# A list-scheduled attention and MLP kernel: opening reordered, MLP tiles put forward, second weights in three pieces, last tile split 512+256 on two queues

## The chip, the cores and the metric

The kernel runs on one core of a Trainium2 chip. The metric is the device time of one execution in microseconds (us), as the median of several executions. "Half clock" below means stretches in which the record of the granted TensorE clock is below 1.0; in the trace before it was 0.5 in one such stretch of 3.4 us, from 22.14 to 25.55 us. All runs of this case are on one core, and none was put into a slower state than "fast".

## The reference

```python
# q, k, v: (8, 12, 448, 64) float32;  x: 3584 x 768;  w_in: 768 x 2048;  w_out: 2048 x 768
scores = (1 / sqrt(64)) * q @ k.T                  # per batch and head, 448 x 448
attn   = maximum(scores, 0) ** 2 / 448 @ v
x      = attn.transpose(0, 2, 1, 3).reshape(3584, 768)
h      = x @ w_in
g      = 0.5 * h * (1 + erf(h / sqrt(2)))          # exact gelu
out    = g @ w_out                                 # float32
```

## The kernel before

All matrix products are in bf16; the loads cast on the way (float32 inputs, bf16 tiles). A scheduler written in Python fixes the order of each engine's instructions when the kernel is built. In the trace before TensorE kept to it: it stood 1.28 us, up to 20.45, before transposes whose keys had not landed, with other work behind them. The scheduler keeps a model of when each engine comes free, when a load lands and when a buffer is released, and issues next the operation whose modelled start plus a bias is lowest. So a changed bias, or a changed model of a load, changes the order on every engine. Once the attention of batch 2 begins, TensorE's order is a fixed list that mixes attention of one batch with the MLP of the two before.

```python
T_BIAS = -0.5      # transposes of queries and keys
T_LATE = 0.2       # ... of the second half of batch 0's queries
F1_BIAS = 0.2      # MLP tiles of the first half of batch 0
F1B_BIAS = 0.2
RELU_DVE = 0.36    # extra cost of relu on DVE instead of ACT
DMA_FREE = 4.0
LEAD = 5           # MLP tiles of batch 1 ahead of the first scores of batch 2
...
    def commit(self, est, op, eng, dur, lat):        # in class Scheduler
        if eng == "PE" and est < self.COLD: dur, lat = 2 * dur, 2 * lat    # COLD = 18.0
        if isinstance(lat, tuple):                   # a load: (bytes, count)
            t = max(self.dma, est + dur + 1.0)
            self.dma = t + lat[0] / 390e3
            op.done = self.dma + DMA_LAT
...
    sch = Scheduler({"w": 3, "a": NA, "f": 2, "osb": 3})    # score, square, MLP, output buffers
...
    # warm-up of TensorE, before anything has landed
    spin = w_pp.tile([128, 2, NB], F32, tag="w", name="spin")
    for _ in range(45):
        nc.tensor.matmul(spin[:, 0, :128], zero, zero, start=True, stop=True)
...
    # one pair of score blocks: TensorE -> "ps"; ACT (or DVE) relu -> "a_sq"; DVE squares it
            A.activation(ar, ps, AF.Relu, scale=c_att)       # or V.tensor_scalar(...)
            V.tensor_mul(box["a2"][:, :, :used], ar, ar)
...
    # batch 2: permute on DVE, transpose by DMA, and a gate that holds back later loads
    for g in range(G):
        add_pk(2, g, g + 1, bias=T_TWO)
        add_pq(2, g, g + 1, bias=T_TWO)
    add_T_dma(2, [[]] * 7)
    add_gate(2)
    add_wout(0)                                      # second weights, first half
    add_wout(1)                                      # ... second half
...
    # an output tile: 128 tokens x 768, as two halves of 384 (ND), stored by SP
    for kf in range(KF):
        nc.tensor.matmul(po[:, :ND], hT[pr][:, kf, bass.ts(t, 128)],
                         wout_sb[:, kf, bass.ts(n, ND)], start=(kf == 0), stop=(kf == KF - 1))
    copy(e, osbs[pr, t][:, bass.ts(n, ND)], box[0][:, :ND])
    ...
    nc.sync.dma_start(rows[c, p0 : p0 + m, :], osbs[pr, t][...])
```

Names in the profile: `tp` are transposes on TensorE of queries `nq` and keys `nk`, `ps` scores, `pav` the attention product, `psh` the first MLP product and `pso` the second. Batches 0 and 1 are transposed on TensorE, later ones by DMA (`kT<-pk`, `qT<-pq`).

## Time and profile before

| | before |
|---|---|
| time, median of 3 | 396.78 us (396.65 to 398.15) |
| profiled execution | span of 395.7 us, of which TensorE is busy 381.9 |
| last copy ends, to the end of the span | 391.27, 4.4 us |

The page of a profile gives busy times and 40 slices of the span. The waits of an engine list what ended its idle time. The timeline gives, in order, start, duration, engine, line and tile of each group, with the idle time before it in brackets. The lines on which the argument rests are shown in the prediction below. In the trace before, 16 matmuls of 384 columns take 2.60 us, 162.5 ns each (the last copies of 384 columns start at 388.11 and 390.71), and the issue of a store takes about 0.4 us.

### The profile page before, as it was taken

The page shows a single profiled execution, that of the slowest core. Times are in us where ns is not written, and L with a number is a line of the kernel's source. Part 1 is how long each engine was busy: PE and PEld are TensorE (multiplying, and loading weights), DVE is VectorE, ACT ScalarE, POOL GpSimd, SP SyncE. Part 2 cuts the span into 40 slices and gives each one's busy share as a digit, 9 for nine tenths or more (in the row PEclk, how much of TensorE's full clock was granted, in tenths as well). Part 3 has the DMA queues.
Part 4 walks back from the last instruction along what each step waited for, and adds up shares of the span by engine and source line. Part 5 has one row for each costly group of instructions (what it writes and reads, how often), then busy time and mean ns, then how long its engine had stood idle before and what let it go on. Part 6 is the DMA issues. An engine that isn't in the chain of part 4 may idle for free.

```text
span 395.7 us, 8091 instructions
## 1 busy us (share of the span) xinstructions
PE 381.9 (97%) x3497; PEld 218.1 (55%) x3497; DVE 187.5 (47%) x346; ACT 200.5 (51%) x306; POOL 45.2 (11%) x68
## 2 busy tenths in 40 slices
PE   7689999999999999999999999999999999999994
PEld 6467684455455555555555555555555555555562
DVE  3868963267737345555456345545355352111111
ACT  4969956763534564465635456356626545222200
POOL 8665204000200200020000200000000000000000
PEclk9989999999999999999999999999999999999999
DMA  9999956999996792579119871370111011110122
GB/s 174 194 202 204 200 94 105 211 204 207 159 195 132 116 193 54 112 135 184 42 42 164 125 140 41 65 156 2 42 30 51 0 41 41 40 39 2 41 80 80
DMA packets 69347, 42.94 MB, mean 109 GB/s; under 512 B 37696, under 2 KB 65728, under 8 KB 69312
## 3 DMA queue, kind: packets, MB, share of 16 engines
q0 software_dynamic: 30496, 22.47, 38.2%
q1 hardware_dynamic: 38544, 19.51, 22.5%
q8 instruction: 27, 0.44, 0.4%
q10 hardware_dynamic: 272, 0.46, 0.3%
q14 instruction: 8, 0.07, 0.0%
HBM read 45.61 MB, written 11.01 MB: 143 GB/s over the span
## 4 chain that ended last, share of the span: by engine, by line
PE 79%; DMA 10%; ACT 3%; DVE 3%; SPq 2%; POOL 1%; issue 1%; POOLq 0%
PE pso L665 33%; PE psh L625 32%; DMA nq<-in_q_dram 9%; PE ps L516 7%; PE pav L578 6%; ACT a_sq L528 2%; SPq L479 2%; DMA qT<-pq 1%; DVE a_sq L537 1%; PE tp L447 1%; POOL nk L332 1%; DVE a_sq L530 1%; ACT h_sb L637 1%; DVE xT L299 0%; POOL wout_sb L271 0%
## 5 line engine op out<-in xcount | busy, mean ns | idle before, releaser
L625 PE MATMUL psh<-xT,win_sb 128*128 128x448 bf16 (+1 forms) x864 | 155.9, 334 | 0.0
L665 PE MATMUL pso<-wout_sb,h_sb 128*128 128x384 bf16 x896 | 151.7, 326 | 0.0
L528 ACT ACTIVATE a_sq<-ps 128x896 bf16<-128x896 f32 x143 | 124.7, 916 | 48.8 <-PE ps L516 48.8
L537 DVE TENSOR_TENSOR a_sq<-a_sq 128x896 bf16<-128x896 bf16 (+1 forms) x169 | 100.6, 618 | 55.6 <-ACT a_sq L528 55.6
L665 PEld LDWEIGHTS <-h_sb 128*128 128x128 bf16 x896 | 86.3, 98 | 62.3 <-issue 5.6
L637 ACT ACTIVATE h_sb<-psh 128x448 bf16<-128x448 f32 x128 | 70.2, 549 | 99.0 <-PE psh L625 98.9
L625 PEld LDWEIGHTS <-win_sb 128*128 128x128 bf16 x864 | 82.1, 98 | 66.4 <-issue 9.2
L299 DVE COPY osb<-pso 128x384 f32<-128x384 f32 x56 | 31.2, 557 | 91.5 <-PE pso L665 91.5
L516 PE MATMUL ps<-qT,kT 64*64 64x448 bf16 (+1 forms) x756 | 47.4, 339 | 3.8 <-ACT a_sq L528 2.1
L530 DVE TENSOR_SCALAR a_sq<-ps 128x896 bf16<-128x896 f32 x26 | 28.3, 1090 | 37.5 <-PE ps L516 37.5
L578 PE MATMUL pav<-a_sq,v_sb 64*64 64x448 bf16 (+1 forms) x756 | 36.6, 329 | 0.8 <-ACT a_sq L528 0.8
L516 PEld LDWEIGHTS <-kT 64*64 64x64 bf16 x756 | 19.1, 106 | 24.4 <-issue 17.9
L578 PEld LDWEIGHTS <-v_sb 64*64 64x64 bf16 x756 | 21.1, 107 | 12.4 <-issue 2.1
L301 ACT CAST xT<-pav 128x448 bf16<-128x448 f32 (+1 forms) x27 | 13.3, 491 | 14.4 <-PE pav L578 9.7
L299 DVE CAST xT<-pav 128x448 bf16<-128x448 f32 (+1 forms) x27 | 15.4, 572 | 10.3 <-PE pav L578 5.4
L491 POOL COPY gate<-qT 128x4 bf16<-128x4 bf16 x5 | 0.9, 187 | 161.8 <-DMA qT<-pq 161.8
L248 POOL DMA_DIRECT2D nq<-in_q_dram x14 | 11.6, 828 | 4.4 <-ACT a_sq L528 2.0
L347 POOL DMA_DIRECT2D v_sb<-in_v_dram x14 | 10.6, 758 | 2.2 <-DMA win_sb<-in_moe_w_in_dram 1.2
L332 POOL DMA_DIRECT2D nk<-in_k_dram x13 | 10.0, 770 | 4.1 <-issue 1.2
L383 DVE COPY pq<-nq 112x512 bf16<-112x512 bf16 x36 | 8.3, 287 | 0.5 <-DMA nq<-in_q_dram 0.5
L372 DVE COPY pk<-nk 128x896 bf16<-128x896 bf16 x18 | 6.3, 386 | 1.1 <-DMA nk<-in_k_dram 1.1
L762 PE MATMUL spin<-zero 128*128 128x128 bf16 x45 | 4.6, 299 | 1.0 <-DVE zero L749 1.0
(24 smaller groups left out, 42.0 us busy)
## 6 DMA issues: line engine op xcount, KB each, us to landing
nk<-in_k_dram POOLq DMA_DIRECT2D x5, 672.0 KB, 7.9
nq<-in_q_dram POOLq DMA_DIRECT2D x5, 672.0 KB, 10.6
v_sb<-in_v_dram POOLq DMA_DIRECT2D x5, 672.0 KB, 13.2
wout_sb<-in_moe_w_out_dram POOLq DMA_DIRECT2D x2, 1536.0 KB, 14.7
out_dram<-osb SPq DMA_DIRECT2D x8, 336.0 KB, 2.9
out_dram<-osb SPq DMA_DIRECT2D x8, 288.0 KB, 2.8
v_sb<-in_v_dram POOLq DMA_DIRECT2D x9, 224.0 KB, 8.5
out_dram<-osb SPq DMA_DIRECT2D x8, 240.0 KB, 2.8
```

What stands on the lines that cost most here:

```text
L248: nc.gpsimd.dma_start(nq[b][:, 4 * g0 : 4 * g1, c0 * D : c1 * D], q_view(b, g0, g1, c0, c1))
L299: V.tensor_copy(dst, src)
L301: A.copy(dst, src)
L332: nc.gpsimd.dma_start(nk[b][:, 2 * g0 : 2 * g1], kv_view(k, b, g0, g1))
L516: nc.tensor.matmul(ps[64 * j : 64 * j + 64, e, x * w : x * w + w], kT[r, g, i * 128 + 64 * j : i * 128 + 64 * j + 64], qT[r, 2 * g + j, co ...
L528: A.activation(ar, ps, AF.Relu, scale=c_att)
L530: V.tensor_scalar(ar, ps, c_att, 0.0, op0=mybir.AluOpType.mult, op1=mybir.AluOpType.max,)
L537: V.tensor_mul(box["a2"][:, :, :used], ar, ar)
L578: nc.tensor.matmul(pav[0][o2 : o2 + 64, e, :w], vt[b][r, 2 * g + e, bass.ts(i, D)], box["a2"][r, e, o : o + w], start=(i == 0), stop=(i == ...
L625: nc.tensor.matmul(ph[:, x * n : x * n + n], win_sb[:, kd, bass.ts(m + x, 128)], xT[b][:, kd, c], start=(kd == 0), stop=(kd == KD - 1),)
L637: A.activation(hT[b // 2][:, m : m + nm, o + c.start : o + c.stop], box[0][:, :S].rearrange("p (x n) -> p x n", x=nm), AF.Gelu,)
L665: nc.tensor.matmul(po[:, :ND], hT[pr][:, kf, bass.ts(t, 128)], wout_sb[:, kf, bass.ts(n, ND)], start=(kf == 0), stop=(kf == KF - 1),)
```

## The change

The author had looked at a trace and fitted the scheduler's model of the loads to it, so that TensorE does not stand before keys that have not landed (part 1). More MLP tiles go ahead of and into batch 2 (part 2). The second weights come in 4+6+6 sixteenths instead of 8+8, the first piece ahead of the gate (part 3). The last output tile is 512+256 columns wide and its last two stores go on two queues (part 4).

```diff
-T_BIAS = -0.5
-T_LATE = 0.2
+WOUTS = (4, 6, 6)
+T_BIAS = -0.46
+T_LATE = 0.11
-T_TWO = 0.6
+T_TWO = 0.72
-F1B_BIAS = 0.2
+F1B_BIAS = 0.49
-RELU_DVE = 0.36
-DMA_FREE = 4.0
+RELU_DVE = 0.3
+DMA_FREE = 4.54
-LEAD = 5
+LEAD = 8
-    COLD = 18.0
+    COLD = COLD_END                       # 4.0
...
+        if c1 - c0 < NC and g1 - g0 == G:
+            n += 390e3                    # this load is modelled as 1 us longer
...
+        end = (pr, t) == (B // 2 - 1, 6)
+        c = (slice(0, ND), slice(ND, DM))[n] if not end else (slice(0, NB), slice(NB, DM))[n]
...
-                nc.sync.dma_start(
-                    rows[c, p0 : p0 + m, :], ...
+                (queue.pop(0) if end and n == 1 else nc.sync).dma_start(
+                    rows[k, p0 : p0 + m, cc], ...
...
-                out.append(x[:2] + ([("AV", done)] if done else []) + x[2:4])
+                mid = ("AV", done) if done else ("FFN", None)
+                out.append(x[:2] + [mid] + x[2:4])
...
+    add_wout(0)
     add_steps(steps(1), ATT1_BIAS, True)
...
     add_gate(2)
-    add_wout(0)
     add_wout(1)
+    add_wout(2)
```

More of the change, by code (lines that the diff above doesn't have):

```diff
@@ L52, in cols @@
     return slice(0, S) if half is None else slice(half * HS, half * HS + HS)
+COLD_END = 4.0
 SPIN = 45
@@ L267, in load_win, with load_wout @@
         nc.gpsimd.dma_start(t[1, 64:], w[1, :64])
-    def load_wout(i):
+    def load_wout(kf):
         w = moe_w_out.rearrange("(kf p) d -> p kf d", p=128)
-        nc.gpsimd.dma_start(wout_sb[:, bass.ts(i, KF // 2), :], w[:, bass.ts(i, KF // 2), :])
+        nc.gpsimd.dma_start(wout_sb[:, kf, :], w[:, kf, :])
     pqk = []
@@ L338, in add_q @@
     def add_q(b, g0, g1, c0=0, c1=NC):
-        o = dma(lambda: load_q(b, g0, g1, c0, c1), (g1 - g0) * 4 * KC * (c1 - c0) * 256, war(b))
+        n = (g1 - g0) * 4 * KC * (c1 - c0) * 256
+        if c1 - c0 < NC and g1 - g0 == G:
+            n += 390e3
+        o = dma(lambda: load_q(b, g0, g1, c0, c1), n, war(b))
         for g in range(g0, g1):
@@ L366, in add_wout @@
     def add_wout(i):
-        ld_wout[i] = dma(lambda: load_wout(i), DM * FF * 2)
+        m = sum(WOUTS[:i])
+        kf = slice(m, m + WOUTS[i])
+        ld_wout[i] = dma(lambda: load_wout(kf), DM * 128 * WOUTS[i] * 4)
     def permute_k(copy, g, src):
@@ L659, in add_f2 @@
         box = []
+        end = (pr, t) == (B // 2 - 1, 6)
+        c = (slice(0, ND), slice(ND, DM))[n] if not end else (slice(0, NB), slice(NB, DM))[n]
+        w = c.stop - c.start
         def fn(e):
@@ L665, in fn @@
                 nc.tensor.matmul(
-                    po[:, :ND],
+                    po[:, :w],
                     hT[pr][:, kf, bass.ts(t, 128)],
-                    wout_sb[:, kf, bass.ts(n, ND)],
+                    wout_sb[:, kf, c],
                     start=(kf == 0),
@@ L675, in fn2 @@
                 osbs[pr, t] = opool.tile([128, DM], F32, tag="osb", name="osb")
-            copy(e, osbs[pr, t][:, bass.ts(n, ND)], box[0][:, :ND])
+            copy(e, osbs[pr, t][:, c], box[0][:, :w])
         def store(e):
-            j = 128 * t
+            queue, j = [nc.scalar, nc.sync], 128 * t
+            cc = c if end else slice(0, DM)
             while j < 128 * t + 128:
                 bb, r = divmod(j, S)
-                c, p0 = divmod(r, KC)
+                k, p0 = divmod(r, KC)
                 m = min(KC - p0, 128 * t + 128 - j)
@@ L686, in store @@
                 )
-                nc.sync.dma_start(
-                    rows[c, p0 : p0 + m, :], osbs[pr, t][j - 128 * t : j - 128 * t + m, :]
+                (queue.pop(0) if end and n == 1 else nc.sync).dma_start(
+                    rows[k, p0 : p0 + m, cc], osbs[pr, t][j - 128 * t : j - 128 * t + m, cc]
                 )
@@ L693, in add_f2 @@
         deps = [o for (bb, *_), o in GL.items() if bb in bs] + list(ld_wout.values())
-        op = sch.add((("PE", 2.6, 2.84),), fn, deps, need=("f",), mode="F")
+        d = 2.6 * w / ND
+        op = sch.add((("PE", d, d + 0.24),), fn, deps, need=("f",), mode="F")
         F2[pr, t, n] = op
         ev = sch.add(
-            e_copy(ND, 1)[:1], fn2, [op], frees=("f",), need=("osb",) if n == 0 else ()
+            e_copy(w, 1)[:1], fn2, [op], frees=("f",), need=("osb",) if n == 0 else ()
         )
-        if n == 1:
-            sch.add((("SP", 0.3, 2.5),), store, [ev], frees=("osb",))
+        if n == 1 or end:
+            sch.add((("SP", 0.3, 2.5),), store, [ev], frees=("osb",) if n == 1 else ())
         return op
@@ L867 @@
         for kind, x in slot:
-            pe_q.append(AV[x] if kind == "AV" else QK[x])
+            if kind == "FFN":
+                pe_q.append(stage[0].pop(0)[1])
+            else:
+                pe_q.append(AV[x] if kind == "AV" else QK[x])
         if n < per * len(stage):
```

## The prediction

> **What bounds the kernel now.** The engines are PE (TensorE), DVE (VectorE), ACT (ScalarE), POOL and SP. I read the page's busy table and 40 slices first, for the bound; the waits of the matrix engine, for what interrupts it; its instructions in order of time at the opening; the table by stretches, for what paces the stage; last the end.
>
> ```profile
> PE 381.9 (97%) x3497; PEld 218.1 (55%) x3497; DVE 187.5 (47%) x346; ACT 200.5 (51%) x306; POOL 45.2 (11%) x68
> ...
> PE   7689999999999999999999999999999999999994
> ```
>
> TensorE is the bound: busy 381.9 of 395.7 us, and only the first slices and the last are not full. The 13.8 us that are missing are all that this change can aim at, because it removes no matmul: both programs have 6996 TensorE rows.
>
> ```profile
> PE ps L516 <- ACT a_sq L528: 2.1, 4, 0.7
> PE tp L422 <- DMA nk<-in_k_dram: 2.0, 2, 1.3
> ...
> PE ps L516 <- DMA qT<-pq: 0.9, 1, 0.9
> ```
>
> Of these, 2.0 us are waits for keys to land, 2.1 us waits for ScalarE to empty score buffers, and 0.9 us one wait for the transposed queries of batch 3.
>
> ```profile
> 20.45 0.58 PE L422 MATMUL tp<-ident,nk 128*64 128x128 bf16 x14 [1.28 <-DMA nk<-in_k_dram]
> 21.49 0.58 PE L447 MATMUL tp<-ident,nq 112*64 112x112 bf16 x16 [0.45 <-DMA nq<-in_q_dram]
> 22.00 1.25 PE L516 MATMUL ps<-qT,kT 64*64 64x224 bf16 x24
> ...
> 23.70 2.21 PE L625 MATMUL psh<-xT,win_sb 128*128 128x224 bf16 x12
> ```
>
> Up to 20.45 us TensorE stands (1.28 us) before transposes of batch 1 whose keys have not landed, with other work queued behind them. Then its clock halves: the first MLP tile takes 2.21 us, later ones 1.32.
>
> ```profile
> 10.00:20.00 10.00, 6.37 (x186) 4.60 (x184) 8.59 (x17) 9.10 (x16) 6.63 (x11) 1.00 1.47 194
> 20.00:25.00 5.00, 4.09 (x70) 3.13 (x71) 3.23 (x6) 3.15 (x4) 3.00 (x5) 0.71 1.25 205
> 25.00:30.00 5.00, 5.00 (x121) 4.00 (x122) 3.40 (x8) 3.84 (x6) 3.36 (x5) 0.94 1.29 199
> ```
>
> Columns: stretch, length, then busy us of PE, PE's weight loads, DVE, ACT, POOL, the clock, DMA. From 10 to 20 us DVE and ACT are busy 8.6 and 9.1 of 10: emptying the score buffers paces this stage, not landings. From 20 to 25 us both have 1.8 us to spare.
>
> ```profile
> 87.44 7.32 SPq L471 DMA_TRANSPOSE kT<-pk  x3
> 94.85 1.01 SPq L687 DMA_DIRECT2D out_dram<-osb  x2
> 95.96 5.99 SPq L479 DMA_TRANSPOSE qT<-pq  x4
> ```
> ```profile
> 103.45 0.57 PE L516 MATMUL ps<-qT,kT 64*64 64x448 bf16 x8 [0.94 <-DMA qT<-pq]
> ...
> 105.66 7.97 PE L665 MATMUL pso<-wout_sb,h_sb 128*128 128x384 bf16 x48
> ...
> 386.10 5.98 SPq L687 DMA_DIRECT2D out_dram<-osb  x4
> ...
> 390.71 0.56 DVE L299 COPY osb<-pso 128x384 f32<-128x384 f32 x1 [2.04 <-PE pso L665]
> ```
>
> Batch 3 waits 0.94 us for its transposes, which a store had delayed by 1.01. At the end the last copy stops at 391.27, its two stores are issued by 392.08, and the span ends at 395.7: a tail of 4.4 us.
>
> [...] from the clock column, (1-0.71)x5 + (1-0.94)x5 = 1.75 us of full clock lost, which is half of some 3.5 us. [...] the trace has 16 in 2.60 us, 162.5 each. [...] The trace shows that time as about 0.4 us per store (two between 391.27 and 392.08). [...]
>
> **The change part by part.**
>
> *1. The opening.* From the block of 48 output matmuls at 105.66 us on, both orders on TensorE are the same up to the last tile, so the gain is the difference in reaching that block. The new order transposes keys of batch 1 after one MLP tile instead of before, and puts there the last late query transpose, 16+24 score matmuls and that tile. What can go: waits for landings 0.77 (key group 1) + 1.28 + 0.45 = 2.5 us, and the half clock, 1.75. What stays: six waits of 0.42 to 0.47 for ACT, as nothing lightens ACT or DVE (per pair of score blocks 0.81 ACT + 0.53 DVE, or 1.0 + 0.53 DVE). I walked the new order by hand with durations and landings of this trace (keys of batch 1 at 20.45, queries at 21.49). TensorE reaches its first MLP tile at about 19.5 instead of 23.7, but this is not 4 us of gain: after it the new order has only two MLP tiles, where the old one has four, before the last attention product of batch 0, and the buffers make it wait about 2 us more between 25 and 29, where the old order has none. At 38.99 the old order has just finished the last transposes of batch 1; mine has at that time five score blocks (0.19 each), an attention product (1.33) and some 0.3 of switching more. **Gain 2.5 us.** The landing waits and the clock would be 4.25; 1.75 is given back.
>
> *2. Eight MLP tiles ahead instead of five, one more put into the first group of batch 2.* In the old order TensorE meets batch 2 at 65.04, 0.6 us after its transposes (64.43). 2.5 earlier, it would wait 1.9. Three more tiles of 1.14 us cover 3.4, so no wait. Splitting the four score blocks two and two removes the 0.75 us wait of the fourth for a buffer at 66.55. The 0.17 at 93.42 I also count as gone. **Gain 0.9.**
>
> *3. Second weights in 4+6+6 instead of 8+8.* A quarter (768 KB of bf16) now goes before the gate, into the stretch 50 to 64 us where the DMA is hardly used. At the 207 to 211 GB/s of that load it takes 3.7 us, and everything behind the gate comes that much earlier: the queries of batch 3, and their transposes, now also ahead of the store (1.0). TensorE comes 3.4 earlier (parts 1 and 2), the transposes 4.7, so **the wait of 0.94 ends**. The first output product needs the last piece at about 80.7 and should have it at about 79.5: a margin of 1 us.
>
> *4. The last tile.* Its matmuls take as long. The last copy is 256 wide instead of 384: 0.14 less. Its two stores go on two queues: one issue of 0.4 less. They carry 128 KB instead of 384: stores of 336 KB land in 2.9 us and of 48 in 2.1, so about 0.6 less. **Gain 1.15.**
>
> Sum: 2.5 + 0.9 + 0.94 + 1.15 = 5.5. I take off 0.4 for waits that a hand walk doesn't find: 5.1, so **391.7 us**, 1.3% less.
>
> **Rivals.** (a) *Landings were all of it.* If the buffers don't make it wait at 25 to 29 us, the opening gives 4.25 and the sum is 7.3: 389.5. For it: ACT and DVE have room from 20 us on. Against it: 8.6 and 9.1 of 10 before. (b) *The half clock comes back.* [...] At half clock in a stage paced by ACT it would cost about 0.7; later, in the full stretch, 1.7: 392.4 to 393.4. (c) *The wait moves.* The early piece of weights runs beside the transposes of batch 2, which slow from 1.3 to 2.4 us each under loads (7.32/3 above); batch 2 or the first output product would then wait 1 to 2 us: 393. (d) *Slower.* Needs over 8 us of new waits; with a full TensorE behind them I see none.
>
> **Range and chances.** 391.7 us, from 389.0 (rival a) to 394.4 (b and c together). Faster by over 2% means under 388.8, more than all I count together with (a) less its margin: 0.10. Slower: 0.01. Within 2%: 0.89.
>
> **What would show it.** Right: no wait for keys of batch 1; the first MLP tile near 19.5 us; new waits for ACT or DVE of 1 to 2 us between 25 and 29; batch 2 and batch 3 without a wait for transposes; the block of 48 output matmuls at about 101.3 instead of 105.66, and a tail after the last copy of about 3.4 instead of 4.4. Wrong: a half clock in the full stretch, a wait for the last weights near 80 us, a wait of the score matmuls for the transposes of batch 2 near 65 us, or any wait between 105 and 370 us.

## The result, and the profile after

| | before | after |
|---|---|---|
| time, median | 396.78 us | 393.66 us (392.91 to 394.22, 4 runs) |
| ratio after / before, fast runs | | 0.9912 (95%: 0.9885 to 0.9940) |
| profiled execution, span | 395.7 us | 391.1 us |

A ratio here is the mean time of one kernel's fast runs over the mean of the other's in the same rounds; so it is not quite the ratio of the medians quoted. The change is 0.9% faster, inside the class "within 2%". The profiled execution after, at 392.91, was the fastest of its four; its span of 391.1 flatters the change by some 0.7 us. The profiled execution before took 397.48 us, 0.7 over its median. So the two profiled spans are 4.6 us apart where the medians are 3.1 apart.

First the page of the kernel after: busy times, and TensorE's 40 slices.

```profile
PE 381.4 (98%) x3497; PEld 217.6 (56%) x3497; DVE 188.1 (48%) x348; ACT 200.3 (51%) x304; POOL 45.7 (12%) x69
...
PE   8789999999999999999999999999999999999996
```

TensorE has the same work as before (3497 matmuls). Nearly all change is in its idle time: 9.7 us for 13.8, where its busy time is 381.4 for 381.9. Line numbers are higher than before, by 7 for the scores (L523 for L516). Its waits after:

```profile
PE ps L523 <- ACT a_sq L535: 1.3, 3, 0.5
...
PE ps L523 <- DVE kT L301: 0.7, 1, 0.7
PE pav L585 <- issue: 0.6, 1, 0.6
PE pav L585 <- ACT a_sq L535: 0.6, 2, 0.3
```

No wait for a landing is left: those for the keys, the queries and the transposes of batch 3 are all gone. In their place are waits for ACT and DVE, and one of a new kind: "issue", where the instruction waited for nothing that the profile shows. The timeline of TensorE in the opening shows where it is:

```profile
19.88 1.32 PE L632 MATMUL psh<-xT,win_sb 128*128 128x224 bf16 x12
...
25.76 0.54 PE L585 MATMUL pav<-a_sq,v_sb 64*64 64x224 bf16 x13
26.95 0.57 PE L585 MATMUL pav<-a_sq,v_sb 64*64 64x224 bf16 x15 [0.65 <-issue]
...
28.26 0.57 PE L523 MATMUL ps<-qT,kT 64*64 64x448 bf16 x8 [0.45 <-ACT a_sq L535]
29.07 0.90 PE L585 MATMUL pav<-a_sq,v_sb 64*64 64x224 bf16 x28 [0.23 <-ACT a_sq L535]
```

The first MLP tile comes at 19.88 at full clock (23.70 at half clock before). But an attention product of 28 matmuls is torn in two after 13, though all that it needs is there. The stretches of the kernel after, with the same columns as in the prediction:

```profile
10.00:20.00 10.00, 7.66 (x220) 5.69 (x221) 9.42 (x21) 9.72 (x16) 7.06 (x11) 1.00 1.47 195
20.00:25.00 5.00, 5.00 (x114) 4.20 (x114) 4.95 (x8) 4.90 (x9) 2.79 (x5) 1.00 1.26 206
25.00:30.00 5.00, 3.65 (x100) 2.39 (x96) 4.34 (x10) 4.49 (x6) 3.37 (x6) 1.00 1.30 201
```

DVE and ACT are now at 9.42 and 9.72 of 10 us, and at 4.95 and 4.90 of 5. TensorE is full from 20 to 25 us, then loses 1.35 us from 25 to 30, where the profiled execution before lost none. The transposes of batch 3 on the SP queue, with the store behind them:

```profile
82.32 7.67 SPq L478 DMA_TRANSPOSE kT<-pk  x3
90.08 5.21 SPq L486 DMA_TRANSPOSE qT<-pq  x4
95.40 14.28 SPq L698 DMA_DIRECT2D out_dram<-osb  x8
```

They start 5.1 us earlier than before (87.44), and the store no longer comes between them. TensorE reaches batch 3 at 100.28 without a wait, and the block of 48 output matmuls, from which both programs have the same order up to the last tile, at 102.49:

```profile
100.28 0.57 PE L523 MATMUL ps<-qT,kT 64*64 64x448 bf16 x8
...
102.49 7.97 PE L675 MATMUL pso<-wout_sb,h_sb 128*128 128x384 bf16 x48
```

And the end:

```profile
385.80 0.69 DVE L301 COPY osb<-pso 128x512 f32<-128x512 f32 x1 [2.90 <-PE pso L675]
...
387.55 0.42 DVE L301 COPY osb<-pso 128x256 f32<-128x256 f32 x1 [1.05 <-PE pso L675]
388.00 0.38 ACTq L698 DMA_DIRECT2D out_dram<-osb  x1
```

The last copy ends at 387.97, so the tail is 391.1 - 387.97 = 3.1 us. The 4.6 us between the two profiled spans split into 105.66 - 102.49 = 3.2 up to the block of 48, 4.4 - 3.1 = 1.3 in the tail, and 0.1 by the narrower last copy.

### The profile page after: what moved, and what is told of

Read it like the earlier page. It is cut to its first block, busy times and chain, and to the rows that moved or that the text cites. A ratio compares the mean times of both kernels' runs of the same rounds, so it can differ in the third digit from the quotient of the medians.

```text
span 391.1 us, 8086 instructions
## 1 busy us (share of the span) xinstructions
PE 381.4 (98%) x3497; PEld 217.6 (56%) x3497; DVE 188.1 (48%) x348; ACT 200.3 (51%) x304; POOL 45.7 (12%) x69
## 4 chain that ended last, share of the span: by engine, by line
PE 94%; ACT 3%; DVE 1%; DMA 1%; issue 0%
PE psh L632 38%; PE pso L675 38%; PE ps L523 9%; PE pav L585 8%; ACT a_sq L535 2%; DMA q<-in_q_dram 1%; PE tp L454 1%; PE tp L429 0%; DVE xT L301 0%; DVE a_sq L544 0%; DVE a_sq L537 0%; ACT xT L303 0%; ACT qT L303 0%; ACT kT L303 0%; DVE kT L301 0%
## 5 line engine op out<-in xcount | busy, mean ns | idle before, releaser
L675 PE MATMUL pso<-wout_sb,h_sb 128*128 128x384 bf16 (+2 forms) x896 | 151.7, 326 | 0.0
L301 DVE COPY osb<-pso 128x384 f32<-128x384 f32 (+2 forms) x56 | 31.2, 557 | 89.4 <-PE pso L675 89.4
L523 PE MATMUL ps<-qT,kT 64*64 64x448 bf16 (+1 forms) x756 | 47.4, 336 | 3.6 <-ACT a_sq L535 1.3
L537 DVE TENSOR_SCALAR a_sq<-ps 128x896 bf16<-128x896 f32 x27 | 29.4, 1089 | 40.8 <-PE ps L523 40.8
L523 PEld LDWEIGHTS <-kT 64*64 64x64 bf16 x756 | 18.9, 105 | 24.6 <-issue 17.6
```

The costliest lines, as they stand in the source:

```text
L301: V.tensor_copy(dst, src)
L523: nc.tensor.matmul(ps[64 * j : 64 * j + 64, e, x * w : x * w + w], kT[r, g, i * 128 + 64 * j : i * 128 + 64 * j + 64], qT[r, 2 * g + j, co ...
L537: V.tensor_scalar(ar, ps, c_att, 0.0, op0=mybir.AluOpType.mult, op1=mybir.AluOpType.max,)
L675: nc.tensor.matmul(po[:, :w], hT[pr][:, kf, bass.ts(t, 128)], wout_sb[:, kf, c], start=(kf == 0), stop=(kf == KF - 1),)
```

## The experiments

Twelve kernels ran, each with five rounds beside the kernel before, in three calls (four to a call, on one chip within a call). The quoted expectations were written before each call and use short names for the theories; the sentence ahead of each says what it was to tell apart. In the table, the last two columns are of the profiled execution: the start of the first scores of batch 2, and the time from there to the block of 48. The start is comparable only among kernels with eight MLP tiles ahead of batch 2, so it is left out for two.

| run | time, median (range, n) | ratio to before (95%) | batch 2 starts | to block of 48 |
|---|---|---|---|---|
| result (changed kernel) | 393.66 (392.91 to 394.22, 4) | 0.9912 (0.9885 to 0.9940) | 67.19 | 35.30 |
| e1_after_again | 393.56 (393.49 to 394.13, 5) | 0.9920 (0.9907 to 0.9934) | 67.83 | 35.26 |
| e2_old_open | 393.34 (392.77 to 393.56, 5) | 0.9909 (0.9896 to 0.9923) | 67.34 | 35.60 |
| e3_no_lead | 394.70 (394.11 to 394.87, 6) | 0.9941 (0.9927 to 0.9956) | - | block at 104.21 |
| e4_old_wout | 394.45 (393.93 to 395.62, 6) | 0.9943 (0.9927 to 0.9958) | 68.44 | 35.43 |
| e5_wide_spin | 392.12 (391.88 to 392.14, 4) | 0.9885 (0.9872 to 0.9898) | 66.48 | 35.26 |
| e6_pad | 396.12 (392.74 to 397.45, 22) | 0.9977 (0.9962 to 0.9993) | 69.07 | 35.26 |
| e7_light_mul (wrong on purpose) | 392.38 (392.08 to 393.30, 4) | 0.9897 (0.9884 to 0.9909) | 65.92 | 36.97 |
| e8_lat_wide | 394.09 (393.52 to 394.25, 5) | 0.9934 (0.9922 to 0.9946) | 67.48 | 35.65 |
| e9_old_open_wide | 393.63 (392.67 to 394.49, 6) | 0.9923 (0.9904 to 0.9942) | 67.46 | 35.26 |
| e10_mid_spin | 393.71 (392.56 to 393.94, 6) | 0.9917 (0.9902 to 0.9932) | 67.11 | 35.26 |
| e11_light_act (wrong on purpose) | 391.89 (391.70 to 392.72, 5) | 0.9885 (0.9871 to 0.9899) | 65.46 | 36.69 |
| e12_tail_only | 395.81 (394.20 to 397.07, 17) | 0.9971 (0.9959 to 0.9983) | - | block at 106.10 |

The kernel before had medians of 396.58 (11 runs), 396.69 (27) and 396.85 (22) in the three calls. From batch 2 to the block of 48, 35.26 us is the time with TensorE full, since five kernels with different openings all have it. The page as a whole cannot tell parts 1 to 3 apart; these two columns can.

**The parts, one at a time (e1 to e4).** My theory after the result: the opening gave less than planned, because emptying the score buffers paces it, and something stops TensorE at 26 us. The rivals: the opening gave its share and another part failed, or the half clock took it.

e1 is the changed kernel again, for its spread.

> The changed kernel unchanged, for more runs on one chip. Theory E (evacuation): the opening's waits are not removed but moved from landings to the emptying of score buffers, so the gain of the opening is mainly the half clock that the kernel before shows. Then runs of this kernel spread with their granted clock: clock 1.0 about 393 us, clock 0.996 (one window of 3.4 us at half clock, 1.7 us of clock lost) 0.9 to 1.7 us longer. Rival L (landings): the clock plays no part, all runs within 0.5 us of each other.

Measured: 393.56 us, so the result repeats. Three runs at a clock of 1.0 took 393.49 to 393.56, two at 0.994 took 393.81 and 394.13: the half clock, where it came, cost 0.3 to 0.6 us. The stop is at the same matmul as in the result, and twice as long, which is the difference between the two profiled spans (391.8 and 391.1):

```profile
27.59 0.57 PE L585 MATMUL pav<-a_sq,v_sb 64*64 64x224 bf16 x15 [1.39 <-issue]
```

e2 gives the scheduler its old constants for the opening, and keeps parts 2 to 4.

```diff
-T_BIAS = -0.46, T_LATE = 0.11, T_TWO = 0.72, F1B_BIAS = 0.49, RELU_DVE = 0.3
-DMA_FREE = 4.54, COLD_END = 4.0, n += 390e3
+T_BIAS = -0.5,  T_LATE = 0.2,  T_TWO = 0.6,  F1B_BIAS = 0.2,  RELU_DVE = 0.36
+DMA_FREE = 4.0,  COLD_END = 18.0, n += 0
```

> The changed kernel with only the opening's constants put back: TensorE's order is that of the kernel before up to the MLP tiles ahead of batch 2. Prediction on record: the new opening is worth 2.5 us, so about 396.2. Theory E: 1.0 to 1.5 us, about 394.9, with landing waits of 2.5 us and buffer waits of 2.5 us in the opening as before. If the opening is worth nothing: 393.7.

Measured: 393.34 us, no slower than e1 (ratios 0.9909 and 0.9920, intervals that overlap). **The new opening is worth nothing in the changed kernel**, where the prediction had 2.5 us. e2 has no stop of the kind "issue", and again waits 1.6 us for keys to land and 1.0 for DVE to free a buffer. Its profiled run had the half clock (11.5 to 14.9 us) and still started batch 2 half a microsecond ahead of e1.

e3 takes part 2 away.

```diff
-LEAD = 8
+LEAD = 5
-                mid = ("AV", done) if done else ("FFN", None)
-                out.append(x[:2] + [mid] + x[2:4])
+                mid = [("AV", done)] if done else []
+                out.append(x[:2] + mid + x[2:4])
```

> The changed kernel with five MLP tiles ahead of batch 2 and none in its first group. Prediction on record: without the three tiles TensorE would wait 1.9 us at batch 2 for its transposes, and 0.75 for a score buffer: about 396.3. From the profile after (transposes of batch 2 in at 62.7, TensorE there at 67.2-3.4=63.8): no wait for transposes, 0.75 for a buffer alone: about 394.4. If the tiles are without effect: 393.7.

Measured: 394.70 us, 1.1 slower than e1. The wait of the fourth score block for a buffer is back (waits for ACT 2.1 us in four waits, the longest 0.75, for 1.3 in three). But no wait for the transposes of batch 2 came, which I had said would be 1.9 us. Of the 1.12 us by which its block of 48 is later than e1's (104.21 and 103.09), 0.55 was already there in the last query transposes of batch 1 (40.74 and 40.19), in an opening of the same order: e3's profile has the half clock from 29.5 to 32.9 us, behind its stop, and e1's has none there. So the profile gives this part some 0.6 us. The times give 1.1, but five of e3's six runs had a clock of 0.994 to 0.996, and two of e1's five; the one at 0.999, 394.11 us, is also 0.6 slower than e1's runs at 1.0.

e4 takes part 3 away.

```diff
-WOUTS = (4, 6, 6)
+WOUTS = (8, 8)
-    add_wout(0)              # ahead of batch 1's steps
...
     add_gate(2)
+    add_wout(0)
     add_wout(1)
-    add_wout(2)
```

> The changed kernel with the second weights in two halves, both behind the gate. Prediction on record: the wait of 0.94 us at batch 3 comes back and the first output product waits for the last weights: 394.6 to 395.5. Rival (the transfer is hidden anyway): 393.7, no wait between 60 and 110 us.

Measured: 394.45 us, 0.9 slower than e1, with intervals that overlap. The profile doesn't show the mechanism in its waits: its stop was longer still (1.7 us of idle TensorE), and the half clock stood behind it (27.8 to 31.2 us). So TensorE was 0.23 later than e1 at the end of the stop and 0.61 at batch 2, and from there to the block it lost only 0.17. Its query transposes of batch 3 started at 93.81, 4.8 us later than in e1 (89.03), and were done just before TensorE came, late, at 101.67. So part 3 does make the transposes 4.8 us earlier. What that saves with an opening on time can be estimated from the landings in e4's trace. The last weights landed at 81.75, and e1 starts the first output product at 81.27; the last queries of batch 3 landed at 101.62, and e1 starts batch 3 at 100.88. An opening like e1's would thus have stood about 0.75 us in e4's order (an estimate).

**What the stop is (e5, e6, e10).** The page of the kernel before lists 27 packets and 0.44 MB on a queue called "instruction", which is 16 KiB each. TensorE has 6994 instructions there (each matmul has a weight load and itself, so two), 259 to a packet, and I counted them in blocks of 256, which is 128 pairs. That fits the traces of the kernel before and of the result: with borders every 128 pairs, counted back and on from the stop after pair 478, there are 27 borders for 27 packets, and each packet starts between 4.7 us before and 3.9 us after its border, the first six 2.7 to 3.9 us after. At the other 26 borders the result has at most 0.1 us from the end of a weight load to the start of the next, at the stop 0.9. The times of the packets are decoded from the traces:

```
one block of 256 TensorE instructions (the third border of the program)
           block    packet on queue      all 256     next block   gap between
           entered  "instruction"        issued by   begins       weight loads
before     22.13    25.06 - 25.95        29.42       29.42        none
result     21.14    24.61 - 25.50        25.95       26.95        1.0
e1         21.04    25.36 - 26.29        25.85       27.58        1.7
e2         21.98    25.20 - 26.17        28.31       28.32        none
e5         21.89    26.02 - 26.95        28.81       28.82        none
e6         22.27    26.53 - 27.42        27.08       28.82        1.7
e10        21.30    25.40 - 26.33        26.33       27.81        1.5
```

In every row with a gap the next block begins 1.3 to 1.5 us after its packet has ended, and the packet ends 4.4 to 5.3 us after the block before it was entered. So from the entry of one block to the start of the next it is 5.8 to 6.6 us in these rows (6.8 and 6.9 in e3 and e4, which stop at the same border). Before, this block lasted 7.3 us; in the rows with a gap, with TensorE full of 64-row matmuls, all 256 are issued in 4.8 to 5.0, and TensorE stands for the rest. That it waits there for the instructions of that packet is my reading (theory F below). In the result the packet had ended 0.45 us before the last of the 256 was issued; what passes in the 1.3 to 1.5 us after a packet no trace shows. The packets start 2.9 to 4.3 us after the block was entered. That the loads delay them is a guess: no run varied the loads, and about 50 us, where a packet starts sooner (in the result 1.04 us after its border at 52.27), the result moves as much by DMA (209 GB/s from 50 to 53 us, 206 from 20 to 25). All this is read from traces, so I made the stop go or move.

e5 warms TensorE up with 11 matmuls of 512 columns instead of 45 of 128: 68 fewer instructions, so the border falls later in the program, behind a wait for buffers.

```diff
-SPIN = 45
+SPIN = 11
-        nc.tensor.matmul(spin[:, 0, :128], zero, zero, start=True, stop=True)
+        nc.tensor.matmul(spin[:, 0, :], zero, zero[:, None, :].to_broadcast([128, 4, 128]), ...)
```

> The changed kernel with its 45 warm-up matmuls of 128 columns replaced by 11 of 512: the same work otherwise, but 68 TensorE instructions fewer ahead of the opening. Theory F (instruction fetch): TensorE stands 0.65 to 1.8 us in the middle of an attention product near 26 us [...] the new opening uses one block up in 4.8 us where the old one takes 7.3. With the border moved by 68 instructions the block falls on slower instructions, the stop goes or shrinks below 0.3 us, and the time falls by 0.6 to 1.7: 392.0 to 392.9 against 393.56. Rival (the stop belongs to that attention product or its data): the stop stays at the same matmul, 393.5.

```profile
25.79 0.86 PE L585 MATMUL pav<-a_sq,v_sb 64*64 64x224 bf16 x28
26.60 0.29 PE L523 MATMUL ps<-qT,kT 64*64 64x224 bf16 x4
27.41 1.01 PE L523 MATMUL ps<-qT,kT 64*64 64x448 bf16 x12 [0.52 <-ACT a_sq L535]
```

Measured: 392.12 us, 1.4 faster than e1, and the product of 28 matmuls is whole. Batch 2 starts 1.35 earlier. This is the fastest correct kernel of the study.

e6 is the control: 7 wide matmuls and 38 tiny ones (8 columns), so the number of instructions, and with it the border, is that of the changed kernel.

```diff
+SPIN = 7       # wide, as in e5
+    for _ in range(45 - SPIN):
+        nc.tensor.matmul(spin[:32, 0, :8], zero[:, :32], zero[:, :8], start=True, stop=True)
```

> The control of the run before: 7 wide warm-up matmuls and 38 tiny ones, so the count of TensorE instructions is that of the changed kernel again, with a warm-up as short. Theory F: the stop of 0.65 to 1.8 us is back at the same matmul, 393.3 to 393.8. Rival (the wider warm-up itself helps): no stop, as the wide warm-up.

```profile
26.89 0.54 PE L585 MATMUL pav<-a_sq,v_sb 64*64 64x224 bf16 x13
28.83 0.57 PE L585 MATMUL pav<-a_sq,v_sb 64*64 64x224 bf16 x15 [1.40 <-issue]
```

Measured: the stop is back between the same two matmuls. The time, 396.12 us, is 2.6 worse than e1, more than the stop accounts for, and spread over 4.7 us. Its profiled run had the half clock from 8.5 to 15.3 us, but runs at about 396 had a clock of 1.0 too. That is not explained; e6 speaks for the place of the stop, not for its price.

e10 takes 34 instructions away (28 matmuls of 208 columns), which should move the stop by 34 instructions: past the 15 matmuls that were left of the product (30 instructions) and 2 matmuls into the scores behind it.

```diff
-SPIN = 45
+SPIN = 28
-        nc.tensor.matmul(spin[:, 0, :128], zero, zero, start=True, stop=True)
+        nc.tensor.matmul(spin[:, 0, :208], zero, zero[:, None, :104].to_broadcast([128, 2, 104]), ...)
```

> The changed kernel with 28 warm-up matmuls of 208 columns: 34 TensorE instructions fewer, half of the shift of the wide warm-up. Theory F says where the stop goes: to the second pair of the 4 score matmuls after that attention product (row 958 of this order), and how long: the block before it is entered near 21.5, the next one is usable some 6.2 us later, 27.7, TensorE reaches the border near 26.7, so a stop of 0.5 to 1.5 us; as 0.5 us of buffer wait follows there anyway, the time is 0.2 to 0.9 over the wide warm-up, 392.3 to 393.0. Rival: no stop, or one in the attention product.

```profile
26.33 0.28 PE L523 MATMUL ps<-qT,kT 64*64 64x224 bf16 x2
27.81 0.47 PE L523 MATMUL ps<-qT,kT 64*64 64x224 bf16 x6 [1.20 <-issue]
```

Measured: the stop is after 2 score matmuls, just there. In all six traces with a stop (result, e1, e3, e4, e6 and e10), exactly 478 pairs of weight load and matmul come before it. **That settles that the stop goes with the count of instructions, and not with a buffer, a semaphore or a kind of matmul.** The time was a miss: the runs fell into two groups, 392.6 and 392.8 us at a clock of 0.999, and 393.7 to 393.9 at 0.994 to 0.995; the median is in the slower one. The profiled run is of the faster group, so why the half clock costs 1.1 here and 0.3 to 0.6 in e1 is open.

e9 is the control for the old opening, which has no stop, so e5's edit should give it nothing: e2's constants with e5's warm-up.

> The control on the other side: the old opening (393.34 before) with the wide warm-up. Theory F: the old opening had no stop for instructions, so there is nothing to gain: 393.0 to 393.6, and the new opening then beats it by about 1.2 us when both have the wide warm-up. Rival (a wide warm-up is good for any order): 392.1, as fast as the new opening.

Measured: 393.63 us, no gain over e2 (393.34). So the 1.4 us of e5 are the stop, and not a better warm-up. And with the stop out of both, the new opening is better than the old by 1.0 to 1.2 us (e5 against e2, by the ratios and by the medians; they ran in different calls) to 1.5 (e5 against e9).

**What paces the rest of the opening (e7, e11, e8).** Both controls below give wrong results on purpose, in batches 0 and 1 only, and both start from e5. In e7, DVE squares 32 columns of each block instead of up to 448.

```diff
-            def fn_mul(e_, box=box, used=used):
+            def fn_mul(e_, box=box, used=used, light=blocks[0][0] < 2):
+                if light: used = 32
```

> Wrong result on purpose: the wide warm-up, and in batches 0 and 1 VectorE squares only 32 columns of each score tile; all orders stay. Theory E (the rest of the opening's waits are for score buffers to be emptied): DVE is relieved of some 0.4 us per tile, the waits of TensorE before 32 us fall from about 4 us to 2 to 3, and the time falls by 0.5 to 1.5 against the wide warm-up: about 391.3. Rival L (landings pace it): no change against the wide warm-up.

e11 lets ACT empty only 32 columns of each score buffer; DVE multiplies a piece of the transposed keys instead, so that the squares have their old length.

```diff
+                if e_ == "ACT" and light is not None:
+                    A.activation(ar[:, :, :32], ps[:, :, :32], AF.Relu, scale=c_att)
```

> Wrong result on purpose: the wide warm-up, and in batches 0 and 1 ScalarE empties only 32 columns of each half of a score tile (VectorE multiplies old keys instead, at the same length); all orders stay. Theory A (what is left of the opening's waits is ScalarE alone, as relieving VectorE gained nothing): TensorE's waits for ACT before 32 us, 3.3 us with the wide warm-up, fall below 1.5, and the time falls by 1 to 2.5 us, to about 390.5. Rival L (landings): no change against 392.1. Rival (VectorE takes over as the pace): 0 to 0.7 less, with the waits named for DVE.

By their times neither gains: 392.38 and 391.89 us against 392.12 of e5. The two columns of the table say more. Batch 2 starts 0.56 earlier in e7 and 1.02 earlier in e11 than in e5 (one profile each). In the stretch from 10 to 20 us of e11 ACT fell from 9.72 to 3.91 us:

```profile
10.00:20.00 10.00, 7.62 (x216) 6.02 (x213) 9.48 (x19) 3.91 (x14) 6.73 (x10) 1.00 1.47 195
```

but DVE stayed at 9.48, and the waits went over to it. What was gained was then lost on the way to the block of 48 (36.69 instead of 35.26 us). DVE's next work there is to permute batch 3's keys. First e5, then e11, at that point of DVE's timeline:

```profile
82.01 0.69 DVE L379 COPY pk<-nk 128x896 bf16<-128x896 bf16 x2 [0.85 <-DMA nk<-in_k_dram]
```
```profile
82.51 0.70 DVE L379 COPY pk<-nk 128x896 bf16<-128x896 bf16 x2 [2.37 <-DMA nk<-in_k_dram]
```

DVE waits 2.4 us for the keys in e11, and the squares of batch 2 stand behind that copy in its fixed order, so that TensorE later waits for DVE:

```profile
90.92 0.39 PE L523 MATMUL ps<-qT,kT 64*64 64x448 bf16 x4 [0.89 <-DVE a_sq L540]
```

So the keys of batch 3, behind the second weights, look like the next bound: a faster opening than e5's does not pass through to the end here. That is read from one profile each, and not tested: the keys came 0.50 us later than in e5, and the wait of 0.89 is the larger part of the 1.43 us that e11 lost, not all. e7 shows the same (a wait of 0.9 for DVE at 91.67). The first look at the times alone would have called the engines innocent. Lightening both engines was not tried.

e8 was an attempt to beat e5: the scheduler's model of a landing shortened, which gives another order.

```diff
-DMA_LAT = 2.13
+DMA_LAT = 1.5
```

> A try at a better opening: the wide warm-up, and the scheduling model told that a load is there 1.5 us after its last byte instead of 2.13 [...], which moves MLP tiles and transposes of batch 1 forward. If waits for score buffers can be filled with them: 0.5 to 1.0 faster than the wide warm-up, about 391.7. If they only move: the same. If transposes now meet keys that have not landed: up to 1 slower.

Measured: 394.09 us, 2.0 slower than e5. Batch 2 starts 1.0 later, after more waits for ACT (1.5 and 1.3 us) and with the half clock from 12.1 to 15.6 us; 0.4 more goes on the way to the block. A miss: that constant isn't free to be lowered.

**The tail alone (e12).** The kernel before with part 4 only.

> The kernel before with the last tile alone split 512+256 on two queues. Prediction on record: 1.15 us less, of it 0.14 in the last copy, 0.4 in one issue, 0.6 in the bytes; the profile after shows 4.42 to 3.13 us from the last copy's end to the span's end. Expected 395.3 to 395.6 against about 396.6, with the same tail of about 3.1 us. If the last bytes of the wide half hold the end up instead: under 0.5 us.

Measured: ratio 0.9971, so 0.29% of 396.85, 1.15 us. In its profile the last copy ends at 391.58 of 394.7 us: a tail of 3.1, as after. With the old order of weights it still has the wait of the kernel before for the transposed queries, longer, and one for the last weights, since its opening happened to be faster:

```profile
PE ps L523 <- DMA qT<-pq: 1.5, 1, 1.5
...
PE pso L675 <- DMA wout_sb<-in_moe_w_out_dram: 0.7, 1, 0.7
```

The first is the wait that part 3 was to end, and after the change neither of the two is left.

This trace also shows the old opening at full clock, where the profiled execution before had the half clock from 22.1 to 25.6 us. The start of batch 2, first before, then e12:

```profile
65.04 0.76 PE L516 MATMUL ps<-qT,kT 64*64 64x448 bf16 x12
```
```profile
64.12 0.76 PE L523 MATMUL ps<-qT,kT 64*64 64x448 bf16 x12
```

It is 0.92 us earlier there, and yet the block of 48 comes no earlier (106.10, before 105.66): the two waits take it all back. With the old order of weights an earlier batch 2 did not get through to the block.

## Why the prediction was right or wrong

The time, 393.66 us, lies inside the range (389.0 to 394.4) and in the class that had 0.89. The gain is 3.1 us where the sum said 5.1: the missing 2 us are nearly all in one step.

1. **The opening: the step that failed.** "Gain 2.5 us" measured 0 (e1 against e2). The landing waits did go, the clock stayed full in the profiled execution, as said, and the waits did move to ACT and DVE. Two things were missed. The hand walk never counted instructions: in the full stretch that it found from 20 to 25 us TensorE issued a block of 256 in 4.8 us and then stood for 0.65 to 1.7 us (result, e1, e4), a stop that goes with the count of instructions (e6, e10) and was worth 1.4 us (e5). And without the stop the opening gave 1.0 to 1.5 and not 2.5 (e5 against e2 and e9). Most of that second miss is likely the starting point: the walk set out from an execution 0.7 us over the median, whose half clock had cost the old opening about 0.9 (65.04 against 64.12 in e12, one profile each). The walk itself was about 0.4 too fast: it put the first MLP tile at 19.5 and the block of 48 at 101.3, and they came at 19.88 and, without the stop, at 101.74 (e5). No rival named such a stop. The sentence "the buffers make it wait about 2 us more between 25 and 29" had the size of the loss (1.35 us) nearly right and its cause half wrong: 0.65 was the stop, 0.68 was buffers.
2. **The half clock.** Rival (b) put it at 0.7 to 1.7 (estimates; the trace before lost 1.75 us of full clock), and what brings it about was not shown. Runs of e1 that had it were 0.3 to 0.6 slower, runs of e10 1.1. It came in some runs of nearly every kernel. In the changed kernel it doesn't explain the missing gain, since e1's runs at full clock took 393.5. But behind the stop it put e3's profile back by 0.8 us and e4's by 0.4 against e1's, and so blurs what parts 2 and 3 are worth.
3. **MLP tiles ahead: right in sum, wrong in a reason.** Predicted 0.9; measured 1.1 by the times and some 0.6 by the profile and by the runs at full clock (e3). The buffer wait of 0.75 was the gain. The wait of 1.9 us for the transposes of batch 2 that the three tiles were to cover did not appear without them: the transposes had moved forward too (the gate behind them opened at 62.77 instead of 64.49).
4. **Weights in three pieces: right in mechanism.** The transposes were to come 4.7 us earlier and came 4.8 earlier (e4 against e1); the wait of 0.94 is gone. The size, 0.94, agrees with the 0.9 of the times, but that interval is wide, and e4's profile puts most of its own loss into the opening; the landings in e4 give about 0.75 (an estimate, above). Rival (c) did not occur: no wait at batch 2 or at the first output product. But the stretch from 50 to 64 us was misread as one where "the DMA is hardly used": the share of the DMA was 0.60 to 0.90 from 54 to 64. The early piece was issued at 43.9 and landed at 55.5.
5. **The last tile: right.** Predicted 1.15; measured 1.15 alone (e12). That the two agree to the digit is luck: the interval of e12 is 0.7 to 1.6 us, and the tail was to be 3.4 and was 3.1. The last tile's matmuls took 3.45 + 1.75 = 5.2 us, as long as two halves of 384 columns took before (2 x 2.60).

The parts as measured, 0 + (0.6 to 1.1) + (0.2 to 0.9) + 1.15, make 2 to 3.2; the changed kernel gained 3.0 in the same call. The block of 48 was to come at 101.3 and came at 102.49. In e5, without the stop, it came at 101.74. (The 6996 rows of the prediction are 6994: the page lists 3497 matmuls and 3497 weight loads.)

Open: why e6 is so slow and so spread; why the runs of e10 (and of e9, 392.7 to 394.5) fall into two groups; why the instruction packets start so late in the opening (2.9 to 4.3 us after a block was entered); and whether lightening ACT and DVE together, with earlier keys for batch 3, would give more.

## What to carry to other kernels

In a stage of many short matmuls, count instructions as well as microseconds: here TensorE stood for 0.65 to 1.7 us where it had issued a block of 256 in about 4.8 us and the next began 5.8 to 6.9 us after that block was entered, and 68 instructions fewer ahead of it (a warm-up of 11 wide matmuls instead of 45 narrow ones) moved the border to where TensorE waited for a buffer anyway, and gained 1.4 us. Measure the parts of a change one at a time, since a sum in the right range can hold a part that is worth nothing. When an experiment doesn't move the end, compare markers along the way before calling its cause innocent: e11 was 1.0 us ahead at batch 2 and lost it again at the next landing.
